# A split-precision MLP behind attention: products in the order of their terms, other buffers for late weights, global scores in pairs, and a scaling moved to ScalarE

## Chip, cores and metric

The kernel runs on one core of one Trainium2 chip. The metric is the device time in microseconds (us) of one execution. The engines are TensorE (PE in the profile, its weight loads PEld), VectorE (DVE), ScalarE (ACT), GpSimd (POOL) and SyncE (SP), whose queue issues most of the transfers.

## What is computed

Local and global attention over 8 batches of 8 heads, and an MLP on its output. Each of 512 local queries sees the 32 global keys and the local keys within 32 positions; each of 32 global queries sees all 544 keys.

```python
s_g = scale * np.matmul(q_g, k_all.transpose(0, 1, 3, 2))
out_g = np.matmul(sm(s_g), v_all)
s_ll = scale * np.matmul(q_l, k_l.transpose(0, 1, 3, 2))
mask = np.abs(pos[:, None] - pos[None, :]) <= window     # window = 32
...
a_l = sm(np.concatenate([s_lg, s_ll], axis=-1))
out_l = np.matmul(a_l, np.concatenate([v_g, v_l], axis=2))
...
x = np.ascontiguousarray(attn_out.transpose(0, 2, 1, 3)).reshape(B * S, H * D)   # 4352 x 512
h = x @ w_in                                             # 512 x 2048
g = h * (1.0 / (1.0 + np.exp(-h)))
return (g @ w_out).astype(np.float32)                    # 2048 x 512
```

The weights come as 64-bit floats, q, k and v as 32-bit floats.

## The kernel before

**Tiles.** The 4352 rows of x are 34 row tiles of 128: 32 of local queries (batch, quarter of the sequence) and 2 of global queries. The MLP works through them in 12 blocks n, ten of three tiles and two of two. For each block it goes over 16 slices f of 128 of the 2048 hidden columns. `first_layer(n, f)` makes h (128 x 384), `second_layer(n, f)` adds the slice's product to one output tile per row tile (out0, out1, out2, one PSUM bank each). The second layer of a slice is emitted after the first layer of the next slice.

**Split products.** Each operand is a sum of a high part, rounded to float32r, and the rest: x is xh + xl, a weight w_hi + w_lo, the activated slice gh + gl. A product is three matmuls, high x high, high x low, low x high. The first layer takes them for each of four chunks c of the contraction in turn (L581, 12 matmuls of 384 columns); the second for each row tile in turn (L603, L604, L605, 9 matmuls of 512 columns). Between the two, ScalarE takes a tanh of h (L587), VectorE makes t = (tanh + 1) x h (L588), ScalarE rounds it to gh (L590), VectorE subtracts to get gl (L591).

**Weights.** A slice has two halves of 512 columns, for w_in and w_out. `fetch_weights` (L193, on SyncE) brings a half in as words; `join_words` puts the 64-bit words together into a float32: L209 on ScalarE, L211 (shift) and L212 (combine) on VectorE. `split_weights(f)` makes w_hi on ScalarE (L221) and w_lo on VectorE (L222). Three slices are joined and two split before block 0; the rest is done inside block 0. At slice f of block 0 the code first joins up to slice f + 2, then fetches, then splits slice f + 1, then emits the first layer of f. The raw second halves of slices 8 to 15 stand in the attention's tiles qk and klo (two buffers each), cut in two pieces of 256 columns; the joined slice f is in the tile ws{f+1}, whose last user, w_lo of f + 1, comes when it has been split; w_hi of f is in wh{f}.

**Attention** for later blocks is cut into 128 steps k (a row tile and a pair of heads), which a list of due times puts in order; `fill` emits the next ones between the matmuls of the MLP in proportion to its progress. A step: scores on TensorE (float32 for k < 28 at L348; three-term float32r after that at L350, L351), masked minimum on VectorE (L355), exp on ScalarE (L359), the sums' reciprocals on VectorE (L361, L362), then head 0 scaled on ScalarE (L363) and head 1 on VectorE (L364). From step 12 on the probabilities are transposed by DMA: GpSimd separates the halves of the words (L374), SyncE stores them (`away`, L379) and reads them back transposed (L383). Then TensorE multiplies by v (L425), two heads on the two halves of the array's columns. Global scores of a head pair (`g_scores`) are two matmuls of 272 columns; for batches 0 and 1 in float32 (L256) into the partitions 0 to 63 of two PSUM tiles, each copied out by ScalarE (L257).

**Order.** TensorE's order is the order of the code. The other engines' instructions are placed by a scheduler, but what is inside `hold(...)` (transfers, joins, splits) keeps its order. The output is stored from SyncE's queue for the first and the last block and from ScalarE's for the others (L612 to L615).

Of the kernel before, what the change touches and what calls it, by code (L numbers as in the profile page):

```python
# [12 lines left out]
I32 = mybir.dt.int32  # L13
# [3 lines left out]
ALU = mybir.AluOpType  # L17
# [30 lines left out]
SINGLE = 12  # L48
SCRATCH = 8
FETCH, LOOK = 5, 3  # L50
FIRSTW = {4: 2, 5: 2, 6: 1, 7: 1, 8: 1, 9: 1, 10: 1, 11: 1}
JOINS, SPLITS = (9.0, 9.6, 10.2, 10.8, 11.4, 12.0), (12.1, 12.7)

# [15 lines left out]
def attention_moe_kernel(ctx: ExitStack, tc: tile.TileContext, qk0_in, qk_in, v_in, gqk, wts, out):  # L69
# [112 lines left out]
    def fetch_weights(f, half):  # L182
        i = 2 * f + half
        if half and f >= SCRATCH:
            tag, n = ("qk", QW + KW) if f % 2 else ("klo", SKV)
            homes_ = [work.tile([P, n], I32, tag=tag, bufs=BUFS["qk"], name=f"raw_w{i}_{q}")[:, :DM] for q in range(2)]
        else:
            taken.add(f + SCRATCH * half)
            homes_ = [scratch(f + SCRATCH * half, I32, f"raw_w{i}")]
        n = DM // len(homes_)  # L190
        w_raw[i] = [(raw, q * n, n) for q, raw in enumerate(homes_)]
        for raw, c0, n in w_raw[i]:
            hold(nc.sync.dma_start(out=raw, in_=wts[f, :, DM * half + c0 : DM * half + c0 + n].bitcast(I32)))  # L193
# [49 lines left out]
    def g_scores(b, p):  # L243
        did(("scores", b, p), *([("turn", b - 1, p // 2)] if b else []))
        rows = slice(QG * (p % 2), QG * (p % 2 + 1))
        if b < GF:
            raw = state.pop(("graw", p))
        else:
            hi, lo = state.pop(("gqk", p))
            both, kh = hi[:, : 2 * QG], hi[:, 2 * QG : GW + QG]  # L250
        for j, kind in enumerate("so"):
            s = attbank(kind, f"gs{j}_{b}_{p}")
            ks = slice(j * GH, (j + 1) * GH)
            pg = pgs[p // 2][rows, ks]
            if b < GF:
                nc.tensor.matmul(s[:QG, :GH], raw[:, :QG], raw[:, QG:GW][:, ks], start=True, stop=True)  # L256
                nc.scalar.copy(out=pg, in_=s[:QG, :GH])  # L257
            else:
                nc.tensor.matmul(s[:, :GH], both, kh[:, ks], start=True, stop=False)
                nc.tensor.matmul(s[:, :GH], both, lo[:, ks], start=False, stop=True)  # L260
                nc.scalar.copy(out=pg, in_=s[QG:, :GH])
                nc.vector.tensor_tensor(out=pg, in0=s[:QG, :GH], in1=pg, op=ALU.add)
# [73 lines left out]
    def st_scores(k, b, c, pr):  # L336
# [21 lines left out]
        for u in range(2):  # L358
# [2 lines left out]
        nc.vector.tensor_scalar(out=st[:, 4:6], in0=st[:, 2:4], scalar1=1e-9, scalar2=None, op0=ALU.add)  # L361
        nc.vector.reciprocal(out=st[:, 6:8], in_=st[:, 4:6])  # L362
        nc.scalar.activation(p[:, 0, :W], p[:, 0, :W], AF.Copy, scale=st[:, 6:7])  # L363
        nc.vector.tensor_scalar(out=p[:, 1, :W], in0=p[:, 1, :W], scalar1=st[:, 7:8], scalar2=None,  # L364
                                op0=ALU.mult)
        tiles["p", k] = p.rearrange("p u j -> p (u j)")

    def st_halves(k, b, c, pr):
# [203 lines left out]
    def first_layer(n, f):  # L572
# [1 line left out]
        xh, xl = xblk[n]  # L574
        h = ps_h.tile([P, 512], F32, tag="h", name=f"h{n}_{f}")
        i = 0
        for c in range(NCC):
            wh = w_hi[f][:, c * P : (c + 1) * P]
            wl = w_lo[f][:, c * P : (c + 1) * P]
            for wt, x in ((wh, xh), (wh, xl), (wl, xh)):  # L580
                nc.tensor.matmul(h[:, :nt], wt, x[:, c, :nt], start=(i == 0), stop=(i == 3 * NCC - 1))  # L581
                i += 1
        t = two.tile([P, 3 * P], F32, tag="t", bufs=1, name=f"t{n}_{f}")
        gh = two.tile([P, 3 * P], F32R, tag="gh", name=f"gh{n}_{f}")
# [9 lines left out]
    def second_layer(n, f, gh, gl):  # L594
        if f == 0:
            outs[n] = [ps_out.tile([P, DM], F32, tag=f"out{i}", name=f"out{n}_{i}") for i in range(SIZES[n])]
        wh, wl = w_hi[f][:, DM:], w_lo[f][:, DM:]

        last = n + 1 == len(SIZES) and f == NF - 1
        for i in (reversed(range(SIZES[n])) if last else range(SIZES[n])):  # L600
            o = outs[n][i]
            sl = slice(i * P, (i + 1) * P)
            nc.tensor.matmul(o, gh[:, sl], wh, start=(f == 0), stop=False)  # L603
            nc.tensor.matmul(o, gh[:, sl], wl, start=False, stop=False)  # L604
            nc.tensor.matmul(o, gl[:, sl], wh, start=False, stop=(f == NF - 1))  # L605
            fill(1)
        if f == NF - 1:
            done_ = work.tile([P, 3 * DM], F32, tag=f"xh{n % 2}", name=f"o{n}")
            for i in (reversed(range(SIZES[n])) if last else range(SIZES[n])):
                o = outs[n][i]  # L610
                sb = done_[:, DM * i : DM * (i + 1)]
                nc.scalar.activation(sb, o, AF.Copy, scale=0.5)  # L612
                for p0, np_, r in out_rows(sum(SIZES[:n]) + i):
                    queue = nc.scalar if 0 < n < len(SIZES) - 1 else nc.sync
                    queue.dma_start(out=out[r : r + np_, :], in_=sb[p0 : p0 + np_, :])  # L615

    advance(ends[0])
# [2 lines left out]
    for n in range(len(SIZES)):  # L620
        for f in range(NF):
            if n == 0:
                while w_next[0] < 2 * min(NF, f + LOOK):
                    join_weights()
                for g, half in ((f + FETCH, 0), (f + FETCH - (f + FETCH > SCRATCH), 1)):
# [2 lines left out]
            elif f == 0:  # L628
                advance(ends[n])
                now[:] = n, 0  # L630
            while len(w_hi) < NF and len(w_hi) <= NF * n + f + 1:
                split_weights(len(w_hi))
            g = first_layer(n, f)
            fill(SIZES[n])
            if pend is not None:
# [72 lines left out]
```

## Time and profile before

| | us |
|---|---|
| median of three runs (lowest, highest) | 988.7 (986.22, 989.58) |
| the profiled execution | 991.17 |
| its span, first to last instruction | 989.4 |
| PE busy, share of the span | 961.3, 97% |
| DVE busy | 631.6, 64% |
| ACT busy | 577.9, 58% |
| POOL busy | 200.6, 20% |
| mean granted clock of TensorE | 0.993 |

Times are in us unless marked ns. L581 is line 581 of the kernel. A matmul's record is longer than the step to the next one, since matmuls overlap; the step between starts is what one costs in a row. A float32 matmul leaves two records. In rows of the order of time, "x10" stands for ten instructions merged and "[0.47 <-ACT w L209]" for the idle time before it and what ended that. In the list of waits the numbers are us in total, times, and the longest. The 52 to 148 us of the span lie in block 0; the kernel's first 48 us are attention alone.

### The profile page before, as it was taken

Reading aid. Unit: us, or ns where it says so; the run is one execution under the profiler, and the core shown is the slowest. Engines: PE = TensorE matmul, PEld = TensorE weight load, DVE = VectorE, ACT = ScalarE, POOL = GpSimd, SP = SyncE. Lnnn points to the kernel's source line nnn. Section 1 sums busy time; section 2 is a strip of 40 time slices with the busy share of each in tenths; the row PEclk is TensorE's granted clock in tenths of the full one; section 3 lists DMA queues with packets and bytes.
Section 4 is the critical chain, followed back from the end, with each engine's and each line's share of the span. In section 5 each row is a group of like instructions: output and inputs, shape, how many; then the busy total and the mean of one; then the engine's idle time right before and its main releaser. Section 6 shows DMA issues by size and latency. Waiting matters only on the chain.

```text
span 989.4 us, 17458 instructions
## 1 busy us (share of the span) xinstructions
PE 961.3 (97%) x5790; PEld 852.9 (86%) x5790; DVE 631.6 (64%) x1910; ACT 577.9 (58%) x1483; POOL 200.6 (20%) x413
## 2 busy tenths in 40 slices
PE   8989889999999999999999999999999999999997
PEld 6668778999898989998899999988989899889896
DVE  4888886766767667655577667766677565453322
ACT  7977756666556656644566666666566665343332
POOL 2112222122222212111222122212122221120000
PEclk9999899999999999999999999999999999999999
DMA  8699967566664666534656586565665564433000
GB/s 274 231 280 267 237 168 198 159 167 179 180 165 124 196 178 166 162 95 132 169 159 154 150 209 172 144 192 145 174 180 161 151 162 139 129 83 82 1 22 23
DMA packets 190026, 157.33 MB, mean 159 GB/s; under 512 B 128752, under 2 KB 148720, under 8 KB 189936
## 3 DMA queue, kind: packets, MB, share of 16 engines
q1 hardware_dynamic: 185712, 148.61, 55.1%
q10 hardware_dynamic: 4224, 7.60, 2.2%
q8 instruction: 46, 0.75, 0.3%
q14 instruction: 44, 0.36, 0.1%
HBM read 86.44 MB, written 39.32 MB: 127 GB/s over the span
## 4 chain that ended last, share of the span: by engine, by line
PE 79%; DVE 7%; DMA 6%; ACT 4%; issue 1%; SPq 1%; POOL 1%; DVEq 0%; ACTq 0%; POOLq 0%
PE h L581 33%; PE out L603 11%; PE out L605 11%; PE out L604 11%; PE o L425 6%; DMA raw<-in_qk_dram 3%; PE s L350 2%; PE s L351 2%; DMA raw_g<-in_gqk_dram 2%; DVE w L212 1%; DMA away<-halves 1%; DVE w_lo L222 1%; PE s L348 1%; ACT probs L359 1%; PE gt L296 1%
## 5 line engine op out<-in xcount | busy, mean ns | idle before, releaser
L581 PE MATMUL h<-xh,w_lo 128*128 128x384 f32 (+1 forms) x768 | 254.4, 331 | 8.8 <-DVE w_lo L222 8.8
L374 POOL COPY halves<-probs 128x512 uint16<-128x512 uint16 x232 | 153.0, 685 | 514.9 <-ACT probs L363 171.8
L581 PE MATMUL h<-xh,w_hi 128*128 128x384 f32 (+1 forms) x768 | 254.0, 331 | 0.4 <-ACT w_hi L221 0.4
L581 PE MATMUL h<-xl,w_hi 128*128 128x384 f32 (+1 forms) x768 | 252.8, 329 | 0.0
L603 PE MATMUL out<-w_hi,gh 128*128 128x512 f32 x544 | 220.9, 406 | 2.5 <-ACT gh L590 2.3
L605 PE MATMUL out<-w_hi,gl 128*128 128x512 f32 x544 | 215.5, 396 | 2.0 <-DVE gl L591 1.9
L604 PE MATMUL out<-w_lo,gh 128*128 128x512 f32 x544 | 214.6, 394 | 0.0
L587 ACT ACTIVATE t<-h 128x384 f32<-128x384 f32 (+1 forms) x192 | 90.4, 471 | 165.5 <-PE h L581 152.7
L588 DVE SCALAR_TENSOR_TENSOR t<-t,h 128x384 f32<-128x384 f32 (+1 forms) x192 | 101.7, 530 | 113.0 <-ACT t L587 112.4
L581 PEld LDWEIGHTS h<-xh,w_lo 128*128 128x128 f32 x768 | 145.6, 190 | 10.9 <-DVE w_lo L222 10.9
L359 ACT ACTIVATE probs<-probs,st 128x224 f32<-128x224 f32 x244 | 115.8, 476 | 65.0 <-DVE st L355 64.1
L581 PEld LDWEIGHTS h<-xh,w_hi 128*128 128x128 f32 x768 | 145.6, 190 | 8.0 <-ACT w_hi L221 0.9
L581 PEld LDWEIGHTS h<-xl,w_hi 128*128 128x128 f32 x768 | 145.5, 190 | 6.6 <-DVE xl L433 0.2
L591 DVE TENSOR_TENSOR gl<-t,gh 128x384 fp32r<-128x384 f32 (+1 forms) x192 | 109.4, 570 | 43.5 <-ACT gh L590 39.1
L355 DVE CUSTOM_DVE_ANT_0 probs<-s,mask 128x224 f32<-128x224 f32 x244 | 86.2, 388 | 78.9 <-PE s L351 66.7
L590 ACT CAST gh<-t 128x384 fp32r<-128x384 f32 (+1 forms) x192 | 94.4, 492 | 59.5 <-DVE t L588 59.2
L605 PEld LDWEIGHTS out<-w_hi,gl 128*128 128x128 f32 x544 | 102.5, 188 | 30.1 <-DVE gl L591 7.2
L603 PEld LDWEIGHTS out<-w_hi,gh 128*128 128x128 f32 x544 | 103.1, 190 | 22.0 <-ACT gh L590 6.1
L604 PEld LDWEIGHTS out<-w_lo,gh 128*128 128x128 f32 x544 | 103.2, 190 | 12.9
L332 ACT CAST qk<-raw 128x704 fp32r<-128x704 f32 x100 | 77.7, 777 | 25.8 <-DMA raw<-in_qk_dram 21.3
L363 ACT ACTIVATE probs<-probs,st 128x224 f32<-128x224 f32 x122 | 58.7, 481 | 43.4 <-DVE st L362 41.4
L333 DVE TENSOR_TENSOR klo<-raw,qk 128x448 fp32r<-128x448 f32 x100 | 64.5, 645 | 28.4 <-ACT qk L332 26.1
(91 smaller groups left out, 1075.8 us busy)
## 6 DMA issues: line engine op xcount, KB each, us to landing
raw<-in_qk_dram SPq DMA_DIRECT2D x100, 352.0 KB, 3.4
away<-halves SPq DMA_DIRECT2D x116, 256.0 KB, 2.8
vraw<-in_v_dram SPq DMA_DIRECT2D x30, 512.0 KB, 4.7
raw_w<-in_wts_dram SPq DMA_DIRECT2D x24, 512.0 KB, 6.6
raw_g<-in_gqk_dram SPq DMA_DIRECT2D x32, 304.0 KB, 4.2
out_dram<-o ACTq DMA_DIRECT2D x28, 256.0 KB, 3.3
raw<-in_qk_dram SPq DMA_DIRECT2D x28, 240.0 KB, 4.3
raw_w<-in_wts_dram SPq DMA_DIRECT2D x16, 256.0 KB, 3.7
```

Of the source, the lines that this page charges most:

```text
L332: nc.scalar.copy(out=qk, in_=raw)
L355: nc.vector.tensor_tensor_reduce(out=p[:, u, :W], in0=ss[u], in1=mask_of[c], scale=-SCALE, scalar=3.0e38, op0=ALU.add, op1=ALU.min, accum_ ...
L359: nc.scalar.activation(p[:, u, :W], p[:, u, :W], AF.Exp, bias=st[:, u : u + 1], scale=-1.0, accum_out=st[:, 2 + u : 3 + u])
L374: nc.gpsimd.tensor_copy(out=halves[:, :, u], in_=p[:, 2 * P * u : 2 * P * (u + 1)].bitcast(U16).rearrange("p (j h) -> p h j", h=2))
L581: nc.tensor.matmul(h[:, :nt], wt, x[:, c, :nt], start=(i == 0), stop=(i == 3 * NCC - 1))
L587: nc.scalar.activation(t[:, :nt], h[:, :nt], AF.Tanh, scale=0.5)
L588: nc.vector.scalar_tensor_tensor(out=t[:, :nt], in0=t[:, :nt], scalar=1.0, in1=h[:, :nt], op0=ALU.add, op1=ALU.mult)
L590: nc.scalar.copy(out=gh[:, :nt], in_=t[:, :nt])
L591: nc.vector.tensor_tensor(out=gl[:, :nt], in0=t[:, :nt], in1=gh[:, :nt].bitcast(F32), op=ALU.subtract)
L603: nc.tensor.matmul(o, gh[:, sl], wh, start=(f == 0), stop=False)
L604: nc.tensor.matmul(o, gh[:, sl], wl, start=False, stop=False)
L605: nc.tensor.matmul(o, gl[:, sl], wh, start=False, stop=(f == NF - 1))
```

## The change

It has six parts. (1) The first layer takes all four chunks of high x high, then of high x low (xl), then of w_lo x xh; the second layer takes gh x w_hi for all row tiles, then gh x w_lo, then gl x w_hi, but for the last slice of each block, which stays row tile by row tile. (2) In block 0 slice f + 1 is split before the joins and fetches of that slice, not behind them. (3) The raw second halves of slices 8 to 15 stand in ws15, ws14, ws13, klo, ws14, ws15, klo, qk; those in ws tiles come whole, with one transfer. (4) The two float32 matmuls of global scores go to the two column halves of the array, into partitions 0 to 63 and 64 to 127 of one PSUM tile. (5) In steps 12 to 27 ScalarE scales both heads. (6) Of the last block's output, row tile 0 is stored from ScalarE's queue, row tile 1 from SyncE's.

```diff
+PLACES = ("ws15", "ws14", "ws13", "klo", "ws14", "ws15", "klo", "qk")
...
         if half and f >= SCRATCH:
-            tag, n = ("qk", QW + KW) if f % 2 else ("klo", SKV)
-            homes_ = [work.tile([P, n], I32, tag=tag, bufs=BUFS["qk"], name=f"raw_w{i}_{q}")[:, :DM] for q in range(2)]
+            tag = PLACES[f - SCRATCH]
+            if tag in ("qk", "klo"):
+                n = QW + KW if tag == "qk" else SKV
+                homes_ = [work.tile([P, n], I32, tag=tag, bufs=BUFS["qk"], name=f"raw_w{i}_{q}")[:, :DM] for q in range(2)]
+            else:
+                homes_ = [const.tile([P, 2 * DM], I32, tag=tag, name=f"raw_w{i}")]
...
+        if b < GF:
+            s = attbank("so"[p % 2], f"gs{b}_{p}")
+            for j in range(2):
+                nc.tensor.matmul(s[QG * j : QG * (j + 1), :GH], raw[:, :QG], raw[:, QG:GW][:, j * GH : (j + 1) * GH],
+                                 start=True, stop=True)
+            for j in range(2):
+                nc.scalar.copy(out=pgs[p // 2][rows, j * GH : (j + 1) * GH], in_=s[QG * j : QG * (j + 1), :GH])
...
-        nc.vector.tensor_scalar(out=p[:, 1, :W], in0=p[:, 1, :W], scalar1=st[:, 7:8], scalar2=None,
-                                op0=ALU.mult)
+        if KF <= k < ND:
+            nc.scalar.activation(p[:, 1, :W], p[:, 1, :W], AF.Copy, scale=st[:, 7:8])
+        else:
+            nc.vector.tensor_scalar(out=p[:, 1, :W], in0=p[:, 1, :W], scalar1=st[:, 7:8], scalar2=None,
+                                    op0=ALU.mult)
...
-        for c in range(NCC):
-            wh = w_hi[f][:, c * P : (c + 1) * P]
-            wl = w_lo[f][:, c * P : (c + 1) * P]
-            for wt, x in ((wh, xh), (wh, xl), (wl, xh)):
-                nc.tensor.matmul(h[:, :nt], wt, x[:, c, :nt], start=(i == 0), stop=(i == 3 * NCC - 1))
+        for wt, x in ((w_hi[f], xh), (w_hi[f], xl), (w_lo[f], xh)):
+            for c in range(NCC):
+                nc.tensor.matmul(h[:, :nt], wt[:, c * P : (c + 1) * P], x[:, c, :nt], start=(i == 0),
+                                 stop=(i == 3 * NCC - 1))
...
+        terms = ((gh, wh), (gh, wl), (gl, wh))
+        if f < NF - 1:
+            order_ = [(i, j) for j in range(3) for i in range(SIZES[n])]
+        else:
+            order_ = [(i, j) for i in (reversed(range(SIZES[n])) if last else range(SIZES[n])) for j in range(3)]
+        for done_, (i, j) in enumerate(order_, 1):
+            g, w = terms[j]
+            nc.tensor.matmul(outs[n][i], g[:, i * P : (i + 1) * P], w, start=(f == 0 and j == 0),
+                             stop=(f == NF - 1 and j == 2))
+            if done_ % 3 == 0:
+                fill(1)
...
-                    queue = nc.scalar if 0 < n < len(SIZES) - 1 else nc.sync
+                    queue = nc.sync if n == 0 or last and i else nc.scalar
...
             if n == 0:
+                split_weights(f + 1) if 0 < f < NF - 1 else None
                 while w_next[0] < 2 * min(NF, f + LOOK):
                     join_weights()
...
-            while len(w_hi) < NF and len(w_hi) <= NF * n + f + 1:
-                split_weights(len(w_hi))
```

How it moves the instructions is shown at three places in block 0. The lines of the changed kernel are numbered anew: L211, L212, L222, L355, L361, L362, L363, L364, L588, L591 become L216, L217, L227, L364, L370, L371, L372, L376, L599, L602; L374 is the new scaling on ScalarE, L618 all of the second layer. A row has the line, the operation, what it writes and reads, and its shape.

VectorE, before, at slice 3, behind its activation t_3: raw_w and w_899 belong to the joins of slice 5, w_lo_913 is the split of slice 4, st and probs a step's softmax.

```order
L211 TENSOR_SCALAR raw_w_725<-raw_w_725 128x512
L212 SCALAR_TENSOR_TENSOR w_899<-w_899,raw_w_725 128x512
L211 TENSOR_SCALAR raw_w_727<-raw_w_727 128x512
L212 SCALAR_TENSOR_TENSOR w_899<-w_899,raw_w_727 128x512
L222 TENSOR_TENSOR w_lo_913<-w_832,w_hi_912 128x512 x2
L361 TENSOR_SCALAR st_943<-st_943 128x2
L591 TENSOR_TENSOR gl_3_933<-t_3_931,gh_3_932 128x384
L362 RECIPROCAL st_943<-st_943 128x2
L364 TENSOR_SCALAR probs_86<-probs_86,st_943 128x224
```

The same place in the changed kernel (w_897 is the join of slice 5, w_lo_892 the split of slice 4):

```order
L227 TENSOR_TENSOR w_lo_892<-w_831,w_hi_891 128x512 x2
L216 TENSOR_SCALAR raw_w_719<-raw_w_719 128x512
L217 SCALAR_TENSOR_TENSOR w_897<-w_897,raw_w_719 128x512
L216 TENSOR_SCALAR raw_w_721<-raw_w_721 128x512
L370 TENSOR_SCALAR st_933<-st_933 128x2
L602 TENSOR_TENSOR gl_3_923<-t_3_921,gh_3_922 128x384
L217 SCALAR_TENSOR_TENSOR w_897<-w_897,raw_w_721 128x512
L364 ISA probs_85,st_995<-s_992,mask_90 128x224
```

The split of slice 4 has moved ahead of the joins of slice 5, which stand between t and gl as before, and the scaling L364 behind the reciprocal is gone (the new L364 is the old L355).

TensorE, before, two slices on: the end of the second layer of slice 5 (out_0, out_1, out_2 are the row tiles), a score between, and the beginning of the first layer of slice 7.

```order
L605 MATMUL out_0_804<-w_hi_973,gl_5_1063 128x512
L348 MATMUL s_1197<-raw_1024 128x224 x2
L603 MATMUL out_1_805<-w_hi_973,gh_5_1062 128x512
L604 MATMUL out_1_805<-w_lo_974,gh_5_1062 128x512
L605 MATMUL out_1_805<-w_hi_973,gl_5_1063 128x512
L603 MATMUL out_2_806<-w_hi_973,gh_5_1062 128x512
L604 MATMUL out_2_806<-w_lo_974,gh_5_1062 128x512
L605 MATMUL out_2_806<-w_hi_973,gl_5_1063 128x512
L581 MATMUL h_7_1242<-xh_244,w_hi_1125 128x384
L581 MATMUL h_7_1242<-xl_245,w_hi_1125 128x384
L581 MATMUL h_7_1242<-xh_244,w_lo_1126 128x384
```

The same place in the changed kernel, from the second matmul of that second layer on:

```order
L618 MATMUL out_1_798<-w_hi_954,gh_5_1050 128x512
L618 MATMUL out_2_799<-w_hi_954,gh_5_1050 128x512
L357 MATMUL s_1180<-raw_1014 128x224 x2
L618 MATMUL out_0_797<-w_lo_955,gh_5_1050 128x512
L618 MATMUL out_1_798<-w_lo_955,gh_5_1050 128x512
L618 MATMUL out_2_799<-w_lo_955,gh_5_1050 128x512
L618 MATMUL out_0_797<-w_hi_954,gl_5_1051 128x512
L618 MATMUL out_1_798<-w_hi_954,gl_5_1051 128x512
L618 MATMUL out_2_799<-w_hi_954,gl_5_1051 128x512
L591 MATMUL h_7_1222<-xh_242,w_hi_1097 128x384 x4
L591 MATMUL h_7_1222<-xl_243,w_hi_1097 128x384 x4
L591 MATMUL h_7_1222<-xh_242,w_lo_1098 128x384 x4
```

gl is read first by the seventh matmul of a second layer instead of the third, w_lo by the ninth of a first layer instead of the third.

ScalarE, before, between the activations of slices 4 and 5 (the joins L209 are of slice 6, the cast L221 is of slice 5):

```order
L363 ACTIVATE probs_86<-probs_86,st_943 128x224
L209 ACTIVATE w_964<-raw_w_760 128x512
L209 ACTIVATE w_964<-raw_w_762 128x512
L221 CAST w_hi_973<-w_899 128x512 x2
L587 ACTIVATE t_4_992<-h_4_979 128x384
```

The same cast and joins in the changed kernel:

```order
L372 ACTIVATE probs_86<-probs_86,st_933 128x224
L374 ACTIVATE probs_86<-probs_86,st_933 128x224
L226 CAST w_hi_954<-w_897 128x512 x2
L214 ACTIVATE w_960<-raw_w_760 128x512
L214 ACTIVATE w_960<-raw_w_762 128x512
L368 ACTIVATE probs_85,st_995<-probs_85,st_995 128x224
L601 CAST gh_4_983<-t_4_982 128x384
```

The second scaling has come in behind the first, and the cast stands ahead of the joins.

More of the change, by code (lines that the diff above doesn't have):

```diff
@@ L250, in g_scores @@
             both, kh = hi[:, : 2 * QG], hi[:, 2 * QG : GW + QG]
[L251 to L258, printed above, removed]
+        if b < GF:
[6 more added lines that the diff above has]
+        else:
+            for j, kind in enumerate("so"):
+                s = attbank(kind, f"gs{j}_{b}_{p}")
+                ks = slice(j * GH, (j + 1) * GH)
+                pg = pgs[p // 2][rows, ks]
                 nc.tensor.matmul(s[:, :GH], both, kh[:, ks], start=True, stop=False)
@@ L599, in second_layer @@
         last = n + 1 == len(SIZES) and f == NF - 1
[L600 to L606, printed above, removed]
+        terms = ((gh, wh), (gh, wl), (gl, wh))
+        if f < NF - 1:
+            order_ = [(i, j) for j in range(3) for i in range(SIZES[n])]
+        else:
+            order_ = [(i, j) for i in (reversed(range(SIZES[n])) if last else range(SIZES[n])) for j in range(3)]
[5 more added lines that the diff above has]
+                fill(1)
         if f == NF - 1:
```

## The prediction

> **What bounds the kernel now.** I read the page first, then the table of stretches, then the list of who waited for whom on TensorE, then the chain of waits and the order of time in the stretch that these point to.
>
> The page's busy times, its slices, and the stretches (busy us of PE, PEld, DVE, ACT, POOL; then granted clock, DMA share, GB/s):
>
> ```profile
> PE 961.3 (97%) x5790; PEld 852.9 (86%) x5790; DVE 631.6 (64%) x1910; ACT 577.9 (58%) x1483; POOL 200.6 (20%) x413
> DVE  4888886766767667655577667766677565453322
> 52.00:148.00 96.00, 84.96 (x442) 72.35 (x442) 82.12 (x225) 65.70 (x169) 20.62 (x33) 0.95 0.88 239
> 148.00:984.00 836.00, 829.62 (x5038) 745.93 (x5034) 514.91 (x1534) 468.61 (x1185) 169.60 (x338) 1.00 0.53 144
> 70.00:80.00 10.00, 8.05 (x35) 7.65 (x36) 8.82 (x24) 5.04 (x13) 1.24 (x2) 0.83 1.07 283
> 100.00:110.00 10.00, 7.43 (x28) 6.29 (x27) 8.86 (x26) 8.02 (x23) 1.37 (x2) 0.78 0.77 208
> 110.00:120.00 10.00, 9.92 (x64) 8.29 (x64) 7.21 (x20) 5.80 (x17) 1.31 (x3) 0.87 1.13 258
> 130.00:140.00 10.00, 7.99 (x39) 6.60 (x37) 9.61 (x28) 7.49 (x21) 3.09 (x4) 1.00 0.62 186
> ```
>
> From 148 us on TensorE is busy for 829.62 of 836: 6.4 us are all that waits could give back there. The slack lies in 52 to 148 us, the first block of the MLP, in which the weights are also joined and split. There TensorE idles 96 − 84.96 = 11.0 us and ran at 0.95 of its clock (the loss sits in three rows: 1.7 + 2.2 + 1.3 = 5.2 us), while VectorE is busy for 82.12. Who TensorE waited for, from the list of waits (us, times, longest), and the chain there (start, us):
>
> ```profile
> PE h L581 <- DVE w_lo L222: 8.8, 5, 2.6
> PE out L605 <- DVE gl L591: 1.9, 4, 0.8
> DVE w L212 <- ACT w L209: 2.6, 6, 0.5
> 104.88 0.46 DVE gl L591
> 105.34 0.34 DVE w L212
> 105.68 0.61 DVE w_lo L222
> 106.33 3.57 PE h L581 x10
> ```
>
> The chain runs down VectorE's queue, through a join (L212) of a slice that is needed two slices later, to the w_lo that TensorE stands waiting for; the ten matmuls after it then take 3.57 us, because the clock was halved. So VectorE's queue bounds this stage, in its length and in its order. Outside it TensorE does.
>
> **The change, part by part.** Sums are made against the profiled execution: span 989.4 us, 991.17 us in all, 2.5 above the median of 988.7.
>
> *Matmul rate.* The counts stay; only the order differs. In order of time:
>
> ```profile
> 507.19 0.40 PE L603 MATMUL out<-w_hi,gh 128*128 128x512 f32 x1
> 507.42 0.40 PE L604 MATMUL out<-w_lo,gh 128*128 128x512 f32 x1
> 507.66 0.40 PE L605 MATMUL out<-w_hi,gl 128*128 128x512 f32 x1
> 507.89 0.39 PE L603 MATMUL out<-w_hi,gh 128*128 128x512 f32 x1
> 508.58 0.34 PE L581 MATMUL h<-xh,w_hi 128*128 128x384 f32 x1
> 508.75 0.34 PE L581 MATMUL h<-xl,w_hi 128*128 128x384 f32 x1
> 508.93 0.34 PE L581 MATMUL h<-xh,w_lo 128*128 128x384 f32 x1
> ```
>
> Starts lie 0.23, 0.24, 0.23 us apart, though the third step changes the output tile; and 0.17 and 0.18, though the first keeps the stationary operand and the second doesn't. Neither matters in these rows, so I cost the reordering at nothing. One ns on each of 2304 + 1632 matmuls would be 3.9 us, either way; that stays in the range.
>
> *w_lo later needed, earlier made.* In a first-layer group w_lo was needed at the third matmul, now at the ninth: 6 × 0.175 = 1.05 us later. Its split is now issued ahead of a slice's joins. A whole half and one cut in two, from VectorE's order of time:
>
> ```profile
> 94.33 0.34 DVE L364 TENSOR_SCALAR probs<-probs,st 128x224 f32<-128x224 f32 x1
> 94.58 0.42 DVE L211 TENSOR_SCALAR raw_w<-raw_w 128x512 uint32<-128x512 uint32 x1
> 95.48 0.69 DVE L212 SCALAR_TENSOR_TENSOR w<-w,raw_w 128x512 uint32<-128x512 uint32 x1 [0.47 <-ACT w L209]
> 96.08 0.29 DVE L211 TENSOR_SCALAR raw_w<-raw_w 128x256 uint32<-128x256 uint32 x1
> 97.56 1.29 DVE L222 TENSOR_TENSOR w_lo<-w,w_hi 128x512 fp32r<-128x512 f32 x2
> 98.76 0.56 DVE L588 SCALAR_TENSOR_TENSOR t<-t,h 128x384 f32<-128x384 f32 x1
> ```
>
> and from the page's groups the tanh and the making of gl (count, then busy us and mean ns):
>
> ```profile
> L587 ACT ACTIVATE t<-h 128x384 f32<-128x384 f32 (+1 forms) x192 | 90.4, 471 | 165.5 <-PE h L581 152.7
> L591 DVE TENSOR_TENSOR gl<-t,gh 128x384 fp32r<-128x384 f32 (+1 forms) x192 | 109.4, 570 | 43.5 <-ACT gh L590 39.1
> ```
>
> A whole half costs 95.48 − 94.58 − 0.47 + 0.60 ≈ 1.0 us of the queue, so two halves put about 2 us ahead of the split. With 1.05 that is 3 us, more than the longest wait (2.6): all five w_lo waits close as waits. What is late next is gl: between t and gl VectorE has the split (1.2) and the joins (2), in every slice now. gl is ready 0.47 (tanh) + 0.56 (t) + 1.2 + 2 + 0.57 (gl) = 4.8 us after its h; TensorE, which now uses gl in the seventh second-layer matmul of a slice, gets there after 12 × 0.175 + 6 × 0.23 = 3.5 us plus the attention matmuls between, (80 − 16 × 4.2)/16 = 0.8 on average. So waits of some 0.5 us a slice on gl take over, unless VectorE's total shrinks. The total decides, not the label.
>
> *VectorE's total.* Its rows for the scaling in this stage, and the two engines' price of one:
>
> ```profile
> 52.00:148.00 96.00, 4.20 (x12) 0.95 0.88 239
> L363 ACT ACTIVATE probs<-probs,st 128x224 f32<-128x224 f32 x122 | 58.7, 481 | 43.4 <-DVE st L362 41.4
> L364 DVE TENSOR_SCALAR probs<-probs,st 128x224 f32<-128x224 f32 x122 | 41.7, 342 | 3.8
> ```
>
> Twelve of the sixteen moved scalings lie here: 4.20 us by duration, 12 × 0.25 = 3.0 by the step from 94.33 to 94.58. I take 3.5. Of the eight late second halves, all now cut in two, five become whole: 97.56 − 96.08 = 1.48 for two pieces against 1.0, so 5 × 0.4 to 0.5 ≈ 2. VectorE: 82.1 − 5.5 = 76.6. ScalarE gains at most 12 × 0.48 = 5.8 and has 71: not the bound. TensorE's floor: 84.96 − 5.2 (clock) − 1.1 (below) = 79.
>
> *The stage.* At VectorE's share of now (82.12/96 = 0.855) it would last 76.6/0.855 = 89.6 us, a gain of 6.4; at the best ten-microsecond share (0.96) 79.8, TensorE's floor, a gain of 16. VectorE idles 13.9 now; the idle behind late scores goes with TensorE's waits, the 2.6 behind ScalarE's joins stays. I take an idle time of 8.5 to 9: 85.5 us, a **gain of 10.5**. It contains the clock: with no pause of 2 us left, I expect the two half-clock spells (5.2 us) to go.
>
> [...]
>
> *Other homes.* SyncE's order of time, where the fetches of cut halves wait for qk and klo buffers and hold the transposes behind them:
>
> ```profile
> 83.72 6.04 SPq L193 DMA_DIRECT2D raw_w<-in_wts_dram x3
> 89.94 1.23 SPq L383 DMA_TRANSPOSE pt<-away  x1
> ```
>
> A fetch into ws15, ws14 or ws13 finds its tile free or freed three to five slices before. The queue's loads, stores and transposes come earlier; SyncE isn't on the chain above, so I count nothing for it (0 to 1 us). New: the join that opens ws14 or ws15 must wait on ScalarE for VectorE's last join from that tile, about 1 us, twice, with the tanh behind it; covered by ScalarE's 25 us of idle time.
>
> *Global scores.* Float32 matmuls of 272 columns, and the pairs that already run on two column halves, as recorded (two records a matmul):
>
> ```profile
> 40.83 1.13 PE L256 MATMUL gs<-raw_g 128*64 128x272 f32 x4
> 286.80 1.47 PE L425 MATMUL o<-pt,vraw 128*64 128x160 f32 x20
> 52.00:148.00 96.00, 2.26 (x8) 0.93 (x8) 0.95 0.88 239
> ```
>
> Twenty records of 160 columns in 1.47 us are 0.07 each, four of 272 in one half 0.28 each: in pairs about half. That saves 1.1 us of the 2.26 in the stage (counted in the floor), and 6 × 0.5 = 3 us of TensorE before it, where ScalarE is the full engine (10.00 to 20.00: row below). I take 0 there, with −0.8 (steps 12 and 13's scalings now ahead of the first tanh) to +2 as bounds.
>
> ```profile
> 10.00:20.00 10.00, 9.92 (x73) 6.82 (x74) 4.27 (x18) 9.40 (x30) 0.62 (x4) 1.00 1.01 319
> 983.91 2.22 SPq L615 DMA_DIRECT2D out_dram<-o  x5
> ```
>
> *Later waits and the end.* Of the four gl waits (1.9 us) those outside a block's last slice lie under the 4 × 0.23 = 0.9 us by which gl is needed later: gain 1.5 (0 to 1.9). Of the five last stores that SyncE issues in 2.22 us one goes to ScalarE's queue: gain 2.22/5 = 0.45. The first slice of a new block now touches all three output banks within 2 × 0.23 = 0.5 us instead of 6 × 0.23 = 1.4; the evictions have to be done 0.9 us sooner, eleven times: 0 to −1, I take 0.
>
> Sum: 10.5 + 1.5 + 0.45 = 12.4. Profiled, 991.2 − 12.4 = 978.8; against the median 988.7 − 12.4 = **976.3 us**.
>
> **Rivals.**
> 1. *TensorE's floor is reached* (gain 16 in the stage, 18 in all): **971**. For it: VectorE held 9.61 of 10 us in one row. Against: two engines at 77 and 79 of 80 leave no room for a wait on each other.
> 2. *The waits only change their names*: gl takes the place of w_lo and VectorE keeps its share of 0.855. Gain 6.4 in the stage, less what is not won later: 5 to 6 in all, **983**. For it: the 4.8 against 3.5 us above.
> 3. *The half-clock spells stay*, set off by pauses that remain on gl or on scores: 976.3 + 5.2 = **981.5**. Against it: the spell in the chain above follows a w_lo wait. [...]
> 4. *Nothing to measure*: VectorE's 5.5 us are lost again in the prologue and at the block boundaries: **988**.
> 5. *Slower, by ScalarE's queue.* In block 0 the second scaling stands in front of the w_hi casts, the joins and the tanh; if that queue carries the stage, 12 × 0.48 = 5.8 us are added, and nothing is gained: **994**. It decides where ScalarE's share passes VectorE's: now 65.7 to 82.1, then 71 to 77. Against: that distance. For: 9.40 of 10 us in the prologue.
> 6. *The new order costs TensorE*: from 3 ns a matmul (3 × 3.9 = 12 us) the gain is gone; at 5 ns **996**. Against: the equal steps above.
>
> **How the numbers follow.** Forecast 0.50, rival 1 0.19, rival 2 0.15, rival 3 0.04, rival 4 0.05, rival 5 0.05, rival 6 0.02. A measurement of this kernel tells about 0.3% (3 us) from no change. Forecast and rivals 1 to 3 are faster: 0.88; rival 4 is the same: 0.05; rivals 5 and 6 slower: 0.07. The range runs from 969.5 (rival 1, with all 1.9 us of gl waits and the 1 us of SyncE's gone) to 985 (rival 2, with 0.8 us lost before the stage and 1 at the block boundaries): it leaves out rivals 4 to 6 (0.12) and the forecast's tails.
>
> **What would show it.** Right: in the stage that began at 52 us no PE wait on w_lo above 0.5 us, PEclk 1.00 in its slices, VectorE above 0.88 of it and TensorE likewise; the block done some 10 us earlier and 148 to 984 as long as before within 2 us; steps of 0.23 and 0.17 between matmuls. Wrong: a stage as long as now with waits on gl or gh in w_lo's place, ScalarE fuller than VectorE, half-clock spells without pauses, or matmul steps that grew.

## The result, and the profile after

The changed kernel takes 976.5 us (median of four runs, 975.06 to 977.1) beside 988.9 for the kernel before on the same chip: the ratio is 0.9877, with a 95% interval of 0.9856 to 0.9899. The forecast was 976.3. The profiled spans are 974.9 and 989.4.

The busy times and slices of the page, and the stretches that answer to those of before (busy us of PE, PEld, DVE, ACT, POOL; granted clock, DMA share, GB/s):

```profile
PE 950.1 (97%) x5790; PEld 847.1 (87%) x5790; DVE 624.1 (64%) x1884; ACT 584.1 (60%) x1494; POOL 201.7 (21%) x413
DVE  4888976766676677656577567766677566453322
52.00:148.00 96.00, 89.11 (x504) 76.74 (x503) 80.05 (x216) 75.02 (x191) 23.62 (x41) 1.00 0.92 255
70.00:80.00 10.00, 8.48 (x44) 7.15 (x43) 8.54 (x27) 6.89 (x19) 1.17 (x2) 1.00 1.02 316
100.00:110.00 10.00, 7.84 (x39) 6.75 (x39) 8.69 (x24) 8.81 (x23) 2.67 (x4) 1.00 1.02 277
110.00:120.00 10.00, 10.00 (x71) 8.73 (x70) 9.19 (x24) 6.94 (x17) 3.25 (x6) 1.00 1.14 266
130.00:140.00 10.00, 10.00 (x71) 8.73 (x71) 9.35 (x27) 9.24 (x26) 3.27 (x7) 1.00 0.56 150
```

In the same 96 us TensorE has 504 matmul records instead of 442, at clock 1.00 in every row. What it waited for between 46 and 150 us (total, times, longest), and its waits for gl after that:

```profile
PE h L591 <- ACT w_hi L226: 4.0, 4, 1.4
PE s L357 <- DMA raw<-in_qk_dram: 2.2, 2, 1.1
PE out L618 <- ACT gh L601: 0.8, 1, 0.8
PE out L618 <- DVE gl L602: 0.2, 1, 0.2
```

The five waits on w_lo (8.8 us) are gone. In their place stands w_hi, ScalarE's half of the same split: not gl, as the prediction had it. How the w_hi cast comes late is read from ScalarE's order of time, with TensorE's row below it:

```profile
99.67 0.48 ACT L372 ACTIVATE probs<-probs,st 128x224 f32<-128x224 f32 x1 [0.26 <-DVE st L371]
100.06 0.47 ACT L374 ACTIVATE probs<-probs,st 128x224 f32<-128x224 f32 x1
100.43 1.12 ACT L226 CAST w_hi<-w 128x512 fp32r<-128x512 f32 x2
```

```profile
101.08 0.96 PE L591 MATMUL h<-xh,w_hi 128*128 128x384 f32 x4 [0.91 <-ACT w_hi L226]
```

Both scalings of a step (the second is the one that the change moved) stand ahead of the cast, and TensorE begins when the first half is cast, at 101.05 (0.62 us for one of the two). It is the same at all four w_hi waits. But ScalarE's queue isn't full there. Ahead of the longest wait (1.4 us, to 125.68) ScalarE had itself stood still for VectorE's t, with both scalings and the cast behind:

```profile
123.85 0.51 ACT L601 CAST gh<-t 128x384 fp32r<-128x384 f32 x1 [1.58 <-DVE t L599]
```

Matmul steps, in a stretch without waits: three matmuls of 512 columns in 0.69 us, four of 384 in 0.69 to 0.70, so 0.23 and 0.174 each, as before:

```profile
501.22 0.85 PE L618 MATMUL out<-w_hi,gh 128*128 128x512 f32 x3
501.91 0.84 PE L618 MATMUL out<-w_lo,gh 128*128 128x512 f32 x3
502.59 0.84 PE L618 MATMUL out<-w_hi,gl 128*128 128x512 f32 x3
503.27 0.86 PE L591 MATMUL h<-xh,w_hi 128*128 128x384 f32 x4
503.96 0.86 PE L591 MATMUL h<-xl,w_hi 128*128 128x384 f32 x4
504.66 0.88 PE L591 MATMUL h<-xh,w_lo 128*128 128x384 f32 x4
```

Where the 14.5 us between the two spans come from: the first matmul of the first layer starts at 48.3 us before and 48.2 after; the last eviction of block 0 starts at 157.3 and 147.6 (−9.7); from its end to the end of the span 831.5 and 826.7 us pass (−4.8), of which the time behind the last eviction is 4.8 and 3.6 (−1.2). From that first matmul to that eviction TensorE was without a matmul for 11.0 us before and 7.6 after; the half clock cost it 5.1 us there before (clock 0.95; two spells, told at the end) and nothing after (1.00). So of the gain in block 0 about half is the clock.

### The profile page after: what moved, and what is told of

It is laid out like the page before. It is cut to its first block, busy times and chain, and to the rows that moved or that the text cites. A ratio compares the mean times of both kernels' runs of the same rounds, so it can differ in the third digit from the quotient of the medians.

```text
span 974.9 us, 17433 instructions
## 1 busy us (share of the span) xinstructions
PE 950.1 (97%) x5790; PEld 847.1 (87%) x5790; DVE 624.1 (64%) x1884; ACT 584.1 (60%) x1494; POOL 201.7 (21%) x413
## 4 chain that ended last, share of the span: by engine, by line
PE 69%; DMA 3%; ACT 1%; DVE 1%; issue 1%; POOL 0%; SPq 0%; ACTq 0%; POOLq 0%; DVEq 0%
PE out L618 30%; PE h L591 29%; PE o L437 5%; PE s L359 2%; PE s L360 2%; DMA raw<-in_qk_dram 2%; DMA raw_g<-in_gqk_dram 1%; DMA away<-halves 0%; PE gs L268 0%; PE gt L305 0%; PE gs L269 0%; POOL halves L386 0%; ACT qk L341 0%; SPq L395 0%; DVE qk L343 0%
## 5 line engine op out<-in xcount | busy, mean ns | idle before, releaser
L599 DVE SCALAR_TENSOR_TENSOR t<-t,h 128x384 f32<-128x384 f32 (+1 forms) x192 | 101.7, 529 | 108.1 <-ACT t L598 107.4
L618 PE MATMUL out<-w_hi,gh 128*128 128x512 f32 x544 | 164.8, 401 | 2.7 <-ACT gh L601 2.6
L591 PE MATMUL h<-xh,w_hi 128*128 128x384 f32 (+1 forms) x768 | 160.6, 330 | 4.7 <-ACT w_hi L226 4.0
L618 PE MATMUL out<-w_hi,gl 128*128 128x512 f32 x544 | 161.2, 395 | 0.2 <-DVE gl L602 0.2
L618 PE MATMUL out<-w_lo,gh 128*128 128x512 f32 x544 | 161.1, 394 | 0.0
L591 PE MATMUL h<-xl,w_hi 128*128 128x384 f32 (+1 forms) x768 | 158.2, 327 | 0.0
L591 PE MATMUL h<-xh,w_lo 128*128 128x384 f32 (+1 forms) x768 | 158.2, 327 | 0.0
L591 PEld LDWEIGHTS h<-xh,w_hi 128*128 128x128 f32 x768 | 132.7, 188 | 20.6 <-ACT w_hi L226 6.2
L602 DVE TENSOR_TENSOR gl<-t,gh 128x384 fp32r<-128x384 f32 (+1 forms) x192 | 109.6, 571 | 43.6 <-ACT gh L601 39.4
L364 DVE CUSTOM_DVE_ANT_0 probs<-s,mask 128x224 f32<-128x224 f32 x244 | 86.1, 387 | 74.9 <-PE s L360 63.2
L591 PEld LDWEIGHTS h<-xl,w_hi 128*128 128x128 f32 x768 | 132.7, 188 | 0.0
L591 PEld LDWEIGHTS h<-xh,w_lo 128*128 128x128 f32 x768 | 131.3, 188 | 0.3 <-DVE w_lo L227 0.2
L618 PEld LDWEIGHTS out<-w_hi,gl 128*128 128x128 f32 x544 | 100.3, 188 | 22.6 <-DVE gl L602 1.0
L618 PEld LDWEIGHTS out<-w_lo,gh 128*128 128x128 f32 x544 | 100.5, 188 | 21.6 <-issue 0.6
L618 PEld LDWEIGHTS out<-w_hi,gh 128*128 128x128 f32 x544 | 93.5, 189 | 14.8 <-ACT gh L601 5.6
L372 ACT ACTIVATE probs<-probs,st 128x224 f32<-128x224 f32 x122 | 58.6, 480 | 34.1 <-DVE st L371 32.2
```

The source lines that it names most:

```text
L364: nc.vector.tensor_tensor_reduce(out=p[:, u, :W], in0=ss[u], in1=mask_of[c], scale=-SCALE, scalar=3.0e38, op0=ALU.add, op1=ALU.min, accum_ ...
L591: nc.tensor.matmul(h[:, :nt], wt[:, c * P : (c + 1) * P], x[:, c, :nt], start=(i == 0), stop=(i == 3 * NCC - 1))
L599: nc.vector.scalar_tensor_tensor(out=t[:, :nt], in0=t[:, :nt], scalar=1.0, in1=h[:, :nt], op0=ALU.add, op1=ALU.mult)
L602: nc.vector.tensor_tensor(out=gl[:, :nt], in0=t[:, :nt], in1=gh[:, :nt].bitcast(F32), op=ALU.subtract)
L618: nc.tensor.matmul(outs[n][i], g[:, i * P : (i + 1) * P], w, start=(f == 0 and j == 0), stop=(f == NF - 1 and j == 2))
```

## The experiments

Each ratio is to the kernel before on the same chip. Its medians there were 991.8 us (first four kernels), 989.9 (next four) and 992.5 (last four), so ratios are compared, not times. Single executions of one kernel spread over 2 to 11 us; a block's end from one profile is good to a few us. "Block 0 done" is the start of its last eviction: 157.3 before, 147.6 with the whole change.

### Parts alone, and three together

**Part 1 alone**, terms in order in both layers (the diff's edits to the two layers).

> The kernel before with part 1 alone (terms in order, both layers). Theory: TensorE lost its time in block 0 to w_lo that comes late by VectorE's queue, and to the half clock that these waits set off. With w_lo needed 1.05 us later the five waits of 8.8 us keep at most 8.8 - 5 x 1.05 = 3.5 us, none is over 1.6 us, the granted clock stays 1.00 in block 0 (5.2 us back), and gl waits after block 0 go (1.5). Not all of it can be had, since VectorE's work stays at 82 us: 6 to 9 us in all, 980 to 983. Rival 'the total decides': VectorE's work is the same, so waits only change their names and the time stays within 2 us of before after block 0's share, 986 to 988. Rival 'the clock drops by itself': waits shrink but the spells of half clock stay, 984 to 985.

Measured: ratio 0.9919 (0.99 to 0.9937); block 0 done at 152.7, and 828.4 us from there to the end. The waits in block 0:

```profile
PE h L579 <- DVE w_lo L222: 3.3, 4, 1.6
PE s L348 <- DMA raw<-in_qk_dram: 2.2, 2, 1.4
```

As the theory said: 3.3 us on w_lo for 3.5 expected, longest 1.6, and the clock is 1.00 in the stage. The order of the terms alone brings about two thirds of the gain. The rival by which only VectorE's total counts (83.38 us busy here, 82.12 before) is out by its time. What it says of the waits did come in this profile: w_hi (1.5 us), a transposed tile (1.6) and gh (1.4) stand beside w_lo, and TensorE is without a matmul in block 0 for 10.9 us, beside 11.0 before. The 4.5 us by which block 0 is done sooner are the 5.1 of the half clock: with more but shorter pauses (longest wait 1.6 us, for 2.6) there is none. Most executions of the kernel before lose less to it than the profiled one (mean clock 0.996 in the median of 25, 0.993 in that one; 0.998 in the median of the four here), so by time the clock is some 2 us of the 8.

**Part 2 alone**, the split ahead of the joins:

```diff
             if n == 0:
+                split_weights(f + 1) if 0 < f < NF - 1 else None
                 while w_next[0] < 2 * min(NF, f + LOOK):
...
-            while len(w_hi) < NF and len(w_hi) <= NF * n + f + 1:
-                split_weights(len(w_hi))
```

> The kernel before with part 2 alone (slice f + 1 split ahead of the joins). Theory: w_lo is made about 2 us sooner, so the 8.8 us of w_lo waits nearly close and with them the half clock; gl, still needed by the third matmul of a slice and now behind the split and the joins on VectorE, waits instead by some 3 us, and the gl waits after block 0 stay: 981 to 984. Rival 'the total decides': 987 to 989, with gl waits of 6 us or more in place of w_lo's. Rival 'the clock drops by itself': 985.

Measured: 1.0036 (1.0015 to 1.0057), slower; block 0 done at 156.2. The waits in block 0:

```profile
PE s L348 <- DMA raw<-in_qk_dram: 11.2, 5, 4.5
PE h L581 <- DVE w_lo L222: 0.4, 1, 0.4
```

w_lo closes as said, and gl does not take its place. A load of scores does, which no theory had: 11.2 us, longest 4.5, and the half clock behind them still costs 5.1 us (clock 0.83 from 100 to 110 us, 0.66 from 110 to 120; 0.95 in the stage).

**Part 5 alone**, ScalarE scales both heads in steps 12 to 27:

```diff
+        if KF <= k < ND:
+            nc.scalar.activation(p[:, 1, :W], p[:, 1, :W], AF.Copy, scale=st[:, 7:8])
+        else:
+            nc.vector.tensor_scalar(out=p[:, 1, :W], in0=p[:, 1, :W], scalar1=st[:, 7:8], scalar2=None,
+                                    op0=ALU.mult)
```

> The kernel before with part 5 alone (ScalarE scales both heads in steps 12 to 27). Theory: VectorE has 3.5 us less to do in block 0, but in the old order each w_lo still stands behind two joined halves: the w_lo waits shrink by about a third, to 5 or 6 us, one spell of half clock stays, 984 to 987. Rival 'the total decides': 3.5 / 0.855 = 4.1 us shorter, 984.5 or less, in proportion, and more if the clock stays up. Rival 'ScalarE's queue': w_hi, joins and tanh come later by the added scalings, 988 to 994.

Measured: 1.003 (1.0016 to 1.0044), slower, in the range of the third rival. VectorE is down from 82.12 to 77.76 us in the stage and TensorE still waits for w_lo for 8.1 us, now eight times:

```profile
52.00:148.00 96.00, 83.97 (x453) 69.75 (x454) 77.76 (x212) 70.09 (x182) 19.29 (x36) 0.98 0.87 238
PE h L584 <- DVE w_lo L222: 8.1, 8, 2.1
```

Less work for VectorE did not bring w_lo earlier. Block 0 is done only 1 us sooner, and the blocks after it are longer; that they are by ScalarE's queue, as the rival has it, isn't shown. TensorE's waits for gh behind block 0 are 5.6 us here, beside 2.1 before, but the longest (1.8) is at 657.8 us, long after the last moved scaling (161.2), and part 3 alone, which moves none, has 4.2.

**Parts 1, 2 and 5 together** (the three diffs above).

> The kernel before with parts 1, 2 and 5 together, without other homes, paired global scores and the moved store. Theory: nearly the whole gain of the change: no w_lo wait over 0.5 us, clock 1.00, VectorE at 78.6 us instead of 76.6 since the late halves stay cut in two: 977 to 979.5. Rival 'the homes and the pairs carry a good part': 981 to 984, with fetches of cut halves (SyncE) or weights in raw form as the releaser of the waits that are left.

Measured: 1.0024 (1.0 to 1.0048); block 0 done at 159.3. Neither theory: nothing is left of the gain of part 1, and the wait is that of part 2. SyncE's order of time, SyncE's largest wait in the stage, and TensorE's rows:

```profile
81.77 9.93 SPq L193 DMA_DIRECT2D raw_w<-in_wts_dram  x2
95.88 2.90 SPq L193 DMA_DIRECT2D raw_w<-in_wts_dram  x3
103.03 7.23 SPq L193 DMA_DIRECT2D raw_w<-in_wts_dram  x3
110.35 0.39 SPq L310 DMA_DIRECT2D raw<-in_qk_dram  x1
SPq L193 <- DVE w L212: 24.0, 10, 9.1
```

```profile
101.84 1.46 PE L348 MATMUL s<-raw 128*128 128x224 f32 x3 [4.10 <-DMA raw<-in_qk_dram]
114.32 1.69 PE L348 MATMUL s<-raw 128*128 128x224 f32 x4 [3.89 <-DMA raw<-in_qk_dram]
```

And VectorE's, where it stands and when the last of the joins comes:

```profile
103.82 0.39 DVE L355 CUSTOM_DVE_ANT_0 probs<-s,mask 128x224 f32<-128x224 f32 x1 [3.83 <-PE s L348]
104.14 1.29 DVE L222 TENSOR_TENSOR w_lo<-w,w_hi 128x512 fp32r<-128x512 f32 x2
105.34 0.42 DVE L211 TENSOR_SCALAR raw_w<-raw_w 128x512 uint32<-128x512 uint32 x1
109.45 0.42 DVE L212 SCALAR_TENSOR_TENSOR w<-w,raw_w 128x256 uint32<-128x256 uint32 x1
```

This is a circle. SyncE stands in a fetch from 103.03 to 110.26 until a join (109.45) frees a qk or klo buffer; behind the fetch waits the load of a step's scores (110.35), for which TensorE waits to 114.32; and VectorE, in its own queue, stands on the scores (3.83 us for those of 101.84, and 2.83 us for those of 114.32) with the next split and joins behind them. With the joins behind the split, every turn of the circle is late. SyncE stood in fetches for 23.2 us before as well, but never for more than 4.9 at a time, and TensorE's wait for scores was 0.4 us. Where the two pauses for scores (4.10 and 3.89 us) end, the clock is down as well, 0.66 from 100 to 110 us and 0.83 from 110 to 120, which costs 5.1 us in the stage (clock 0.95).

### Other homes, and VectorE's total

**Part 3 added to 1, 2 and 5** (the diff's PLACES and its use).

> Parts 1, 2, 5 and now 3 (other homes); still without paired global scores and the moved store. Theory after the last runs: with the split ahead of the joins, the joins that free qk and klo come later, so SyncE stands in its fetches of late halves (24.0 us in parts 1, 2, 5; longest 9.1) with the loads of the scores behind them, for which TensorE waited 11.4 us. With homes that are free, these waits go: raw waits below 3 us, 977 to 979.5. Rival 'the pairs of global scores and the store carry it': 990 to 995, raw waits as before.

Measured: 0.9866 (0.9805 to 0.9927); block 0 done at 149.0. From 1.0024, the other homes are worth 1.6%, some 15 us (give or take 6, by the two intervals), in this order. Some 5 of them are the half clock, which is gone in this profile (1.00 in the stage, for 0.95). What SyncE and TensorE wait for in the stage:

```profile
SPq L198 <- DVE w L217: 2.5, 3, 1.2
PE s L353 <- DMA raw<-in_qk_dram: 2.3, 2, 1.2
PE h L587 <- ACT w_hi L226: 4.5, 4, 2.0
```

**The same, but in two pieces:**

```diff
-                homes_ = [const.tile([P, 2 * DM], I32, tag=tag, name=f"raw_w{i}")]
+                t = const.tile([P, 2 * DM], I32, tag=tag, name=f"raw_w{i}")
+                homes_ = [t[:, :DM], t[:, DM:]]
```

> As the run with parts 1, 2, 5 and 3, but the five late halves in ws tiles are still fetched, shifted and joined in two pieces of 256 columns. It parts the two effects of the other homes. Theory 'the queue': SyncE waits as little as with whole halves; VectorE has about 2 us more in block 0, half of which shows: within 2 us of the run with whole halves, 977 to 981. Rival 'VectorE's total': the cut pieces were the loss, most of the difference to 995 comes back: 985 or more.

Measured: 0.9894 (0.9838 to 0.995), block 0 done at 148.9: no difference that can be told. The homes work through SyncE's queue, not through VectorE's shorter joins. How much the shorter joins are worth isn't shown: the pieces added only 0.4 us to VectorE's work in the stage (80.29 for 79.91), where 2 were expected.

**Part 3 alone.**

> The kernel before with part 3 alone. Theory: in the old order SyncE's waits on fetches (23 us) end before anything is needed, TensorE waits on w_lo; the waits on fetches go but w_lo stays, VectorE has 2 us less: 986 to 989, w_lo waits of 6 to 9 us and at least one spell of half clock. Rival 'homes are worth something by themselves': 980 to 984.

Measured: 0.9998 (0.9971 to 1.0025). SyncE's 23 us of waits on fetches are gone, TensorE still waits for w_lo:

```profile
PE h L586 <- DVE w_lo L227: 8.4, 8, 2.3
```

As the theory said in time and w_lo waits; a half-clock spell in the stage, also expected, didn't come (the stage's clock is 1.00, the mean of the whole execution 0.997). Without one, block 0 is done at 152.6 in this profile, but 835.8 us follow instead of 831.5. So the same edit is worth nothing in the old order and some 15 us in the new one.

**The whole change without part 5** (VectorE scales head 1 again).

> The changed kernel without part 5 (VectorE scales head 1 in steps 12 to 27 as before). Theory as on record: VectorE gets 3.5 us back, block 0 is 3 to 4 us longer, 979 to 981, waits on w_lo or gl come back by some us. Rival 'ScalarE is the new bound': the w_hi waits (4.0 us) were due to the scalings that stand in front of the casts; without them they shrink to 1 or 2 us and the time stays within 1.5 us of the changed kernel, 975 to 978.

Measured: 0.9891 (0.984 to 0.9942), which can't be told from the whole change, and block 0 done at 147.8. The stage:

```profile
52.00:148.00 96.00, 89.13 (x496) 77.04 (x495) 84.05 (x227) 70.28 (x176) 24.52 (x40) 0.98 0.90 251
PE h L588 <- ACT w_hi L226: 3.8, 3, 2.0
```

VectorE has 84.05 us to do instead of 80.05, TensorE is as busy (89.13 and 89.11). The theory fails: the 3.5 us off VectorE are worth nothing that shows. Of the rival only the time holds: the w_hi waits aren't made by the moved scaling. Differences of some 5 us of time could hide in this interval; the block's end is the finer measure, and it contains a spell of half clock (0.83 from 130 to 140 us, which costs 1.7 us) that the whole change doesn't have.

### One part less, and one step further

**The whole change without part 2.**

> The changed kernel without part 2 (slice f + 1 is split behind the joins and fetches again). Theory: the terms' order leaves 3.3 us of w_lo waits (as in the run with part 1 alone), shorter now by VectorE's 5.5 us less work: w_lo waits of 1 to 3 us, raw waits no larger than with the change since the joins come sooner; block 0 is 1 to 3 us longer: 977 to 980. Rival 'the split ahead of the joins carries the stage': 982 to 985.

Measured: 0.9889 (0.9869 to 0.9908), w_lo waits of 3.4 us (longest 1.4) and raw waits of 1.7; block 0 done at 151.2, 3.5 us later in the profile. In time the difference isn't resolved: 0.0012, about 1 us, by the middles of two intervals that overlap.

**The whole change without part 4** (paired global scores).

> The changed kernel without part 4 (global scores of batches 0 and 1 as two matmuls of 272 columns one after the other). On record: nothing before the stage, 1.1 us of TensorE in it, within the forecast. Theory: block 0 ends 0.5 to 1.3 us later, the rest as it was: 976.5 to 978. Rival 'the pairs carry the difference between parts 1, 2, 3, 5 and the whole': 978.5 to 980.

Measured: 0.987 (0.9848 to 0.9892): nothing, by time. Block 0 is done at 150.3, 2.7 later than with the pairs, more than the theory said; some 1.9 of it is the half clock (0.98 over the 96 us of the stage), and the rest is of the size of the 1.1 us on record. The pairs take 0.6 of the time, 0.68 us for four records where 1.13 stood; two rows of the whole change:

```profile
40.75 0.68 PE L259 MATMUL gs<-raw_g 128*64 128x272 f32 x4
42.41 0.71 PE L437 MATMUL o<-pt,vraw 128*64 128x160 f32 x8 [0.51 <-ACT pt L406]
```

The second row shows what becomes of it at this place in the prologue: TensorE waits 0.51 us for ScalarE.

**The whole change with the second layer as before** (part 1 in the first layer only):

```diff
-        for done_, (i, j) in enumerate(order_, 1):
...
+            nc.tensor.matmul(o, gh[:, sl], wh, start=(f == 0), stop=False)
+            nc.tensor.matmul(o, gh[:, sl], wl, start=False, stop=False)
+            nc.tensor.matmul(o, gl[:, sl], wh, start=False, stop=(f == NF - 1))
+            fill(1)
```

> The changed kernel with the second layer row tile by row tile again (part 1 for the first layer alone): gl is needed by the third matmul of a slice, not the seventh. It tests the step of the prediction that gl comes late next. Theory: in block 0 gl waits of 2 to 5 us come up, after block 0 the 1 to 2 us of gl waits of the kernel before are back (block 9 of 76.2 us instead of 74.3): 979 to 983. Rival 'gl is not late, VectorE has slack': block 0 as in the changed kernel, 977.5 to 978.5 from the later blocks alone.

Measured: 0.9918 (0.9888 to 0.9948). Block 0 is done at 146.6, no later than with the change, and gl costs it 0.2 us: gl is not late there, whichever the order. The difference lies behind block 0: 834.8 us from there to the end instead of 826.7. After block 0 the waits are:

```profile
PE out L614 <- ACT gh L601: 4.9, 6, 1.5
PE out L616 <- DVE gl L602: 1.9, 4, 0.8
```

The 1.9 us on gl are those of the kernel before. Block 9 is 76.3 us long (76.2 before) and 74.3 with the change, and 74.3 or 74.5 in every run with the new order of the second layer.

**The cast one slice sooner**, tried because the wait that is left is on w_hi:

```diff
             if n == 0:
-                split_weights(f + 1) if 0 < f < NF - 1 else None
                 while w_next[0] < 2 * min(NF, f + LOOK):
...
             g = first_layer(n, f)
+            split_weights(f + 2) if n == 0 and f < NF - 2 else None
             fill(SIZES[n])
```

> The changed kernel, but slice f + 2 is split right behind the first layer of slice f, not slice f + 1 at the start of f: on ScalarE the w_hi cast then stands ahead of a step's two scalings. Theory: the wait that is left in block 0 is the cast's place in ScalarE's queue (4.0 us on w_hi, four times): it shrinks to 1 us or less and block 0 is 2 to 3 us shorter, 973.5 to 975. Rival 'VectorE's joins are what the cast waits for': ScalarE then stands in front of them with tanh and gh behind it, waits on gh or h take over: 976 to 980.

Measured: 0.9812 (0.9787 to 0.9837), median 974.0 on a chip where the kernel before takes 992.5; faster than both kernels. Block 0 is done at 142.8. ScalarE's order of time, the stage, and TensorE's largest wait in it:

```profile
96.97 0.62 ACT L226 CAST w_hi<-w 128x512 fp32r<-128x512 f32 x1 [0.34 <-DVE w L217]
97.50 0.48 ACT L598 ACTIVATE t<-h 128x384 f32<-128x384 f32 x1
97.91 0.48 ACT L372 ACTIVATE probs<-probs,st 128x224 f32<-128x224 f32 x1
98.30 0.47 ACT L374 ACTIVATE probs<-probs,st 128x224 f32<-128x224 f32 x1
```

```profile
52.00:148.00 96.00, 92.29 (x526) 80.99 (x525) 81.74 (x225) 78.66 (x198) 24.67 (x42) 1.00 0.97 264
PE s L357 <- DMA raw<-in_qk_dram: 3.4, 3, 1.6
```

The cast now stands ahead of the scalings; w_hi is no longer waited for, though in this row ScalarE itself waits 0.34 us for a join. The same work in another place of two queues is worth 0.65% (0.9877 to 0.9812; the intervals don't touch). In this kernel VectorE's total does come near its limit: it is busy for 29.4 of the 30 us from 100 to 130, beside 29.7 for TensorE. Whether less work for VectorE would show here wasn't tried.

## Why the prediction came out, point by point

- **What bounds the stage.** "VectorE's queue bounds this stage, in its length and in its order": the order is shown (part 1 alone, and the cast one slice sooner), the length is not. "The total decides, not the label" is the step that fails. VectorE's busy time in the stage went from 82.12 to 77.76 us with part 5 alone, and the kernel became slower; with the other parts in place, 84.05 (without part 5) or 80.05 (with it) made no difference that can be told, and neither did cut or whole halves. The prediction's own sign of being right, VectorE busy for over 0.88 of the stage, didn't come either: it is 80.05 of 96 us, 0.83, less than the 0.855 before.
- **The stage's gain.** 10.5 was forecast, and block 0 is done 9.7 sooner. The size was right, and so was the part of it that is the clock (5.2 forecast, 5.1 measured). The working of the rest wasn't: it was made of VectorE's 5.5 us less and an idle share, and it should have been made of arrival times. Part 1 gives 4.5 of it alone in the profile; the rest comes from the other parts together, of which 2 and 5 alone or with 1 cost time until the homes are changed.
- **w_lo closes** as worked out (3.5 left by the order of the terms, 3.3 measured). **What is late next** was wrong: gl waits 0.2 us in all. In the estimate 2 us of joins stood between t and gl in every slice; in the trace gl comes between the two joins, or ahead of the split. Late is w_hi, by its place behind a step's softmax on ScalarE, and that softmax and gh wait for VectorE's order in turn (the 1.58 us above).
- **ScalarE "not the bound"**: true of its total (75.02 of 96 us), and it hid the wait that was left. Rival 5 named the queue and priced the wrong thing, the added scalings: without them the waits are 3.8 instead of 4.0.
- **Other homes counted at 0 to 1**: wrong as a price of its own. SyncE wasn't on the chain of before, but part 2 would have put it there; homes and split had to be priced together. The sum came out since the change makes both.
- **The clock.** Spells gone, as said (1.00 in the stage); rival 3 is out. More on the clock below.
- **Matmul rate, prologue, evictions** 0: right by the steps of 0.23 and 0.174, the start of the MLP at 48.2 for 48.3, and no wait for an eviction in the list.
- **Later waits 1.5 and the end 0.45**: mis-sized. The later part is 4.8 us shorter: 1.2 at the end (3.6 us behind the last eviction in every run with the moved store, 4.2 to 4.9 in the others), 1.7 by gl waits (1.9 to 0.2), 1.9 not assigned. By time the second layer's order is worth 0.9918 − 0.9877, about 4 us.
- **The number.** That 976.3 met 976.5 is luck in part. The sum of 12.4 was made against the profiled execution of 991.17 and then taken from the median; the two profiled executions differ by 14.4, the medians by 12.4.
- **Rivals.** Rival 1's 971, TensorE's floor, was not reached by the change but by the last kernel (988.7 × 0.9812 = 970; TensorE busy for 92.29 of 96 us). Rival 2 was half right: another wait took over, on w_hi and at less than half the size. Rival 6 is out.

What stays open: why part 5 alone is slower by 0.3%, and 1.9 us of the later part.

## What to carry to other kernels

When a wait on an in-order queue is to go, work out when each operand of the waiting instruction arrives and what stands ahead of its maker, rather than how full the maker is: here 4 us of VectorE's work were worth nothing that showed, and a cast issued most of a slice sooner 6 us. Price a reordering together with the buffers that it frees later: the same change of homes was worth nothing in one order and 15 us in the other. And follow every queue that is moved past in a circle (fetch, load, score, softmax, join, fetch), since it is closed only in the new order.

## What was not expected of the hardware

The half clock followed some pauses of TensorE and not others. In the kernel before it came in two spells in block 0, the two rows of 0.50 here; in the stretch of 30.72 us between them the clock is 1.00:

```profile
71.56:74.97 3.41, 3.02 (x9) 3.02 (x10) 2.90 (x8) 1.76 (x4) 1.24 (x2) 0.50 1.02 309
74.97:105.69 30.72, 27.75 (x159) 23.79 (x158) 27.67 (x80) 23.37 (x63) 7.92 (x12) 1.00 0.90 257
105.69:112.52 6.83, 6.18 (x17) 5.61 (x18) 5.74 (x14) 3.48 (x8) 0.64 (x2) 0.50 0.91 255
```

Each began while TensorE stood waiting for w_lo (2.62 us, to 71.95; 2.14 us, to 106.33). In them matmuls of 384 columns start 0.32 us apart and those of 512 columns 0.43, where 0.174 and 0.23 stand elsewhere.

The longest wait doesn't tell when it comes. At 2.0 us the stage's clock was 0.98 without part 5 and 1.00 in parts 1, 2, 3 and 5; at 2.3 us it was 0.98 for the cut pieces and 1.00 with the homes alone.

Measured is that the stage is free of the half clock with the change (longest wait 1.4 us), with part 1 alone (1.6) and with the cast one slice sooner (1.6). That it is the shorter pauses which keep it away was the author's estimate; what decides isn't shown.
